# Block means of the values in four column strips, row units finished block by block, and a new order of work, in an attention and feed-forward kernel

## The chip, the cores and the metric

One core of one Trainium2 chip. The metric is the device time of an execution in microseconds; the times shown are of repeated executions, the profile is of one execution.

## What is computed

The reference, cut to what matters:

```python
def _attn_ref(q, k, v):                      # (2, 8, 768, 64) each
    block, window = (32, 16)
    k_sum = k.reshape(B, H, nb, block, D).max(axis=3)
    v_sum = v.reshape(B, H, nb, block, D).mean(axis=3)
    scores_l = scale * np.matmul(q, k.transpose(0, 1, 3, 2))
    mask_l = np.abs(pos[:, None] - pos[None, :]) < window
    scores_s = scale * np.einsum('bhsd,bhnd->bhsn', q, k_sum) + np.log(block)
    scores_all = np.concatenate([np.where(mask_l, scores_l, -1e9), scores_s], axis=-1)
    a = np.exp(scores_all - np.max(scores_all, axis=-1, keepdims=True))
    a = a / (np.sum(a, axis=-1, keepdims=True) + 1e-09)
    return np.matmul(a, np.concatenate([v, v_sum], axis=2))

def reference(...):
    x = attn_out.transpose(0, 2, 1, 3).reshape(1536, 512)
    g = x @ w_gate                                           # 512 x 1536
    x = (g / (1 + np.exp(-g)) * (x @ w_val)) @ w_out         # 1536 x 512
    h = x @ w2_in                                            # 512 x 2048
    h = np.where(h >= 1, h, np.where(h <= -1, 0.0, (h + 1) ** 2 / 4))
    return h @ w2_out                                        # 2048 x 512
```

So each query sees the keys within 16 positions and one summary per block of 32 keys; the summary of the values is their mean. Two feed-forward layers follow. The weights are stored in 64 bits and are decoded on the chip.

## The kernel before

The 1,536 tokens are three chunks of 512. Chunk 0 is the first two thirds of batch 0; chunks 1 and 2 hold the rest of batch 0 and batch 1. Heads go in four pairs (p).

**Attention** runs by pair and segment of 256 queries: windows of 96 keys and 24 block summaries stand beside each other in `kwin`, so one small matmul gives 120 scores. The steps of a segment are a row of jobs (`STAGES`): `sc` scores on TensorE, `mx` maxima on DVE, `ex` exponentials on ACT, `iv` and `no` normalise, `wt` transposes (tile pt), `pt` copies them (pT), and `av` (`values`, tile px) makes the output of a pair for a chunk. Keys are transposed by `kprep` (pk), queries by `queries` (pq). Where a segment is "wide" (the first `T["wide"]` of them), one exponential covers all four windows and the shift and sums lie on DVE or POOL; else there are four exponentials on ACT. **The means of the values** come from `vmean` (L473): for batch 0 TensorE sums eight windows (`wavg`) and two remaining tiles (`tavg`, loaded by `load_vrest`), ten matmuls for each pair, a job `vm` for each; for batch 1 DVE sums each pair (`vsum`, L468, from `load_vb`) and one matmul finishes it. `vmean_out` copies the 24 x 128 result out, and `vmean_put` spreads it to the four windows of a segment, twice a pair; `av` waits for that.

**Feed-forward.** Products are done in three passes of high and low parts (`PASSES`, `mm3`, L942). Chunk 0 runs through both layers while the weights stream in: a pack of gate and val columns (or of two row units of w_out) is loaded (`raw`), decoded on ACT and DVE (L851, L398, L860), written back to DRAM (`kept`) for later and split into high and low parts (`wA`, L398 and L883). Chunks 1 and 2 are then done together: their column products (tiles qg, qv, qi) use seven forms instead of eight (`FORMS`), and their row products add up in four accumulators y0 to y3 (acc_y), one for each block m of 128. Per layer, all row units f of chunk 1 come first, then those of chunk 2 (`row_jobs`, L1301); a unit does its four blocks one after the other, three 512-column matmuls each. When a chunk's last unit ends, the blocks are copied out: in layer 1 as `yf` (ACT), from which DVE and ACT make the operands of layer 2 (`term_jobs`), in layer 2 to `o` and to DRAM (`put`, `store`, L1027).

**What sets the order.** A planner (`Plan.emit`) places all jobs, one after the other, from a table of numbers `T` (ranks and weights), from the durations that each job names, and from rings of buffers. Each engine then runs its list strictly in that order. Where TensorE would sit idle ahead of a job by the plan, up to ten dummy transposes are put in (`bank`, L296; tile names of the next job, with `ident` alone). All DMAs are issued from SP's queue.

```python
job(("vm", *n), {"PE": 2.2}, t + T["vm"], lambda e, tag: vmean(b, p, tag), ...)       # batch 0
job(("vs", *n), {"DVE": 1.95}, t + T["vs"], lambda *_: vsum(b, p), [("vl", *n)], ...) # batch 1
parts = [(m,) for m in range(KK)] if f == LAST[st] else [(0, 1), (2, 3)]              # row_jobs
```

Of the kernel before, what the change touches and what calls it, by code (L numbers as in the profile page):

```python
# [25 lines left out]
 'urge': 0.0031,  # L26
 'weight': (0.111, 25.399, 0.152, 0.551),
# [3 lines left out]
 'd': (-150.471, 8.098),  # L31
 'load': 18.322,
 'high': 36.678,
 'bits': -9.454,
 'keep': -148.441,
 'read': 301.8,
 'hi': 32.014,
 'lo': 24.389,
 'head_rank': (12.184, 257.325, -210.322, -90.628),
 'start': 65.744,  # L40
 'unit': 2.695,
 'e0': 0.54,
 'a1': (48.053, 1.417),
 'a2': (116.684, 4.853),
 'x': (243.217, 367.077),
 'j': (286.932, 586.062),
 'g': (18.981, 22.593),
 'q': (7.889, 10.225),
 'jr': (169.54, 56.215),
 'jw': (46.283, 26.068),  # L50
 'rw': 1.779,
 'js': (52.141, 283.132),
 'gh': (-149.709, 6.427),
 'gl': 43.009,
 't': -14.215,
 'th': 46.02,
 'tl': -107.144,
 'qp': (2.087, 7.089, 2.273, 9.57, 10.813, 5.604, 7.309),
 'qf': 58.875,
 'qj': -17.592,  # L60
 'qa': 36.904,
 'rs': 40.405,
 'rh': -47.821,
 'x2': 1.227,
 'r2': (-57.746, 112.465),
 'first': (7.961, 21.848),
 'st_q': 10.793,
 'st_qt': -84.924,
 'st_kw': 105.468,
 'st_sc': -56.597,  # L70
 'st_mx': -46.073,
 'st_ex': -56.638,
 'st_iv': -145.71,
 'st_no': 96.909,
 'st_wt': 16.772,
 'st_pt': -59.816,
 'st_av': 6.306,
 'st_xh': -15.454,
 'st_xl': -142.311,
 'kl': -35.186,  # L80
 'kp': 2.73,
 'kt': -15.509,
 'km': 49.836,
 'kc': 98.781,
 'vl': 18.792,
 'vm': -50.669,
 'vs': 47.148,
 'vo': -7.827,
 've': 61.456,
 'ql': -1.492,  # L90
 'wl': 12.107,
 'wide': 8,
 'st_sb': 50.586,
 'st_su': 12.78,
 'seg': 41.24,
 'ko': -84.315}
# [135 lines left out]
def tile_block_attention_ffn(  # L232
# [20 lines left out]
    nc = tc.nc  # L253
# [27 lines left out]
    SLOTS = [f"s{i}" for i in range(22)]  # L281
    XS, XF, US = tuple(SLOTS[:8]), tuple(SLOTS[8:16]), tuple(SLOTS[20:22] + SLOTS[8:16])
    JS = tuple(SLOTS + ["kord", "vb"])
    BANKS, ACCS = ("b0", "b1", "b2", "b3"), ("y0", "y1", "y2", "y3")
    plan = Plan({
        **{r: 1 for r in (*BANKS, *ACCS, *SLOTS)}, "kraw": 2, "kord": 1, "vb": 1, "vr": 1,
# [18 lines left out]
    avg = const.tile([P, NB], F32, name="avg")  # L305
# [26 lines left out]
    averages(avg, 4, NB, 0)  # L332


# [6 lines left out]
    averages(tavg[:, NB:NB + P // BLOCK], BLOCK, P // BLOCK, 0)  # L341
# [113 lines left out]
    SUM_ON_PE = (0,)  # L455
    HELD = 2
    NREST = (S - HELD * SEG) // P

    def load_vrest(b):
        t = vraw[b] = sp.tile([P, NREST, H, D], F32, tag="vb", name="vrest", bufs=1)  # L460
        for j in range(NREST):
            src = v[b, 0, HELD * SEG + j * P]
            nc.sync.dma_start(
                out=t[:, j], in_=bass.AP(src.tensor, src.offset, [[D, P], [S * D, H], [1, D]]))

    def vsum(b, p):
        vr = ap_.tile([4 * NB, 2, D], F32, tag="vr", name="vr", bufs=1)
        nc.vector.tensor_reduce(  # L468
            vr, vraw.pop((b, p)).rearrange("p h t d -> p h d t"), axis=AX.X, op=ALU.add
        )  # L470
        pend["vr", b, p] = vr

    def vmean(b, p, tag):  # L473

        pv = bank(tag, "pv")
        if b in SUM_ON_PE:
            parts = []
            for i in range(HELD * WPS):
# [214 lines left out]
    def head_jobs(b, p, t, banks, after):  # L693
# [720 lines left out]
```

## Time and profile before

| what | us |
|---|---|
| median of 3 runs | 623.97 (622.71 to 625.88) |
| the profiled execution's own time | 623.72 |
| its span, first to last instruction | 621.7 |
| busy: TensorE / weight loads / DVE / ACT / POOL | 607.8 / 494.8 / 486.8 / 364.1 / 96.0 |
| chain that ended last: TensorE's share | 86% |

The span is what the profile sees of the execution; the time has some 2 us more around it. A matmul's record lasts longer than its pace (0.39 us against 0.227 for 512 columns), because matmuls are pipelined; pace is read from the distance of starts. An fp32 matmul that isn't a transpose has two records, one of the split parts has one. Line numbers are those of the kernel before; after the change the same statements stand some 4 to 25 lines higher.

### The profile page before, as it was taken

To read this page: it belongs to the slowest core of one execution; us is meant where nothing else is said; L and a number is where in the kernel's file an instruction comes from. 1 tells how busy PE (TensorE), PEld (TensorE's weight loads), DVE (VectorE), ACT (ScalarE), POOL (GpSimd) and SP (SyncE) were. 2 spreads that over 40 slices of the span, in tenths; PEclk is the share of its full clock that TensorE was granted. 3 is DMA by queue.
4 is the path that set the end of the run, shared out by engine and by line. 5 is a ranking of instruction groups with operands and counts; after the bars stand their busy time and mean duration, and the time that the engine had idled before them with its cause. 6 is when DMAs were issued, how large, how long until landed. Compare 5 with 4: busy or idle time off the path is not lost.

```text
span 621.7 us, 9356 instructions
## 1 busy us (share of the span) xinstructions
PE 607.8 (98%) x3473; PEld 494.8 (80%) x3473; DVE 486.8 (78%) x861; ACT 364.1 (59%) x616; POOL 96.0 (15%) x117
## 2 busy tenths in 40 slices
PE   8798999999999999999999999999999999999997
PEld 6676787777878888888888888888877888888886
DVE  5768998798789898997888875777698788765662
ACT  3698879788787895445454442333177756763222
POOL 6453503241311000003220111000001001000000
PEclk9899999999999999999999999999999999999999
DMA  9999999599993963432111101243200031013411
GB/s 218 293 288 305 266 374 343 186 307 307 328 333 114 371 237 118 153 138 66 69 67 69 67 1 68 69 169 103 99 20 20 0 136 34 2 34 123 148 35 67
DMA packets 76749, 95.50 MB, mean 154 GB/s; under 512 B 36256, under 2 KB 58784, under 8 KB 76704
## 3 DMA queue, kind: packets, MB, share of 16 engines
q1 hardware_dynamic: 76704, 94.91, 47.5%
q8 instruction: 27, 0.44, 0.3%
q14 instruction: 18, 0.15, 0.1%
HBM read 73.92 MB, written 20.97 MB: 153 GB/s over the span
## 4 chain that ended last, share of the span: by engine, by line
PE 86%; DMA 7%; DVE 3%; ACT 3%; issue 1%; SPq 1%; ACTq 0%; DVEq 0%
PE acc_y L942 35%; PE qi L942 11%; PE qv L942 9%; PE qg L942 9%; PE pi L942 7%; DMA raw<-in_moe_w_val_dram 5%; PE pg L942 3%; PE pv L942 3%; DMA qraw<-in_q_dram 2%; PE sc L610 2%; PE pv L486 1%; PE pt L666 1%; PE px L560 1%; PE pq L544 1%; ACT dd L851 1%; ACT dd L398 1%
## 5 line engine op out<-in xcount | busy, mean ns | idle before, releaser
L942 PE MATMUL acc_y<-dd,h 128*128 128x512 f32 x384 | 88.0, 389 | 0.0
L942 PEld LDWEIGHTS acc_y<-dd,h 128*128 128x128 f32 x384 | 72.1, 188 | 15.0
L942 PE MATMUL acc_y<-h,dd 128*128 128x512 f32 x288 | 65.6, 389 | 0.0
L942 PEld LDWEIGHTS acc_y<-h,dd 128*128 128x128 f32 x288 | 54.1, 188 | 11.2
L883 POOL TENSOR_TENSOR wjs<-sj,wjs 128x1024 fp32r<-128x1024 f32 x7 | 17.2, 2456 | 286.6 <-ACT wjs L398 240.6
L398 ACT ACTIVATE dd<-wf 128x1024 fp32r<-128x1024 f32 x23 | 24.3, 1059 | 52.8 <-PE acc_y L942 52.7
L942 PE MATMUL acc_y<-wA,h 128*128 128x512 f32 x192 | 46.0, 390 | 0.0
L942 PE MATMUL qi<-xj,wjs 128*128 128x512 f32 x192 | 45.9, 390 | 0.0
L860 DVE SCALAR_TENSOR_TENSOR wb<-dd 128x1024 int32<-128x1024 int32 x34 | 43.4, 1286 | 2.6 <-ACT dd L398 2.1
L942 PE MATMUL pi<-y,wA 128*128 128x512 f32 x128 | 43.5, 396 | 0.0
L942 PEld LDWEIGHTS qi<-xj,wjs 128*128 128x128 f32 x192 | 36.0, 188 | 7.5
L942 PEld LDWEIGHTS acc_y<-wA,h 128*128 128x128 f32 x192 | 35.9, 188 | 7.5 <-issue 0.2
L851 ACT ACTIVATE dd<-raw 128x1024 f32<-128x1024 f32 x34 | 39.1, 1151 | 4.6 <-DMA raw<-in_moe_w_out_dram 2.9
L883 DVE TENSOR_TENSOR h<-r,h 128x512 fp32r<-128x512 f32 x48 | 33.4, 702 | 3.3 <-ACT h L398 1.9
L942 PE MATMUL acc_y<-h,wA 128*128 128x512 f32 x144 | 35.9, 397 | 0.0
L942 PE MATMUL qi<-xj,wjo 128*128 128x512 f32 x144 | 35.6, 391 | 0.0
L942 PE MATMUL qg<-xj,wjs 128*128 128x512 f32 x144 | 35.6, 389 | 0.0
L942 PE MATMUL qv<-xj,wjs 128*128 128x512 f32 x144 | 35.6, 389 | 0.0
L942 PE MATMUL pg<-x,wA 128*128 128x512 f32 x96 | 34.8, 407 | 0.0
L883 DVE TENSOR_TENSOR dd<-wf,dd 128x1024 fp32r<-128x1024 f32 x28 | 34.1, 1222 | 0.5 <-ACT dd L398 0.4
L883 DVE TENSOR_TENSOR wA<-wb,wA 128x1024 fp32r<-128x1024 f32 x28 | 33.9, 1221 | 0.2
L942 PE MATMUL pv<-x,wA 128*128 128x512 f32 x96 | 34.1, 399 | 0.0
(164 smaller groups left out, 1286.6 us busy)
## 6 DMA issues: line engine op xcount, KB each, us to landing
raw<-in_moe_w_out_dram SPq DMA_DIRECT2D x14, 1024.0 KB, 7.7
raw<-in_moe_w_in_dram SPq DMA_DIRECT2D x16, 512.0 KB, 6.1
wf<-kept_z SPq DMA_DIRECT2D x16, 512.0 KB, 3.2
raw<-in_moe_w_gate_dram SPq DMA_DIRECT2D x12, 512.0 KB, 8.1
raw<-in_moe_w_val_dram SPq DMA_DIRECT2D x12, 512.0 KB, 9.0
kept_g<-wb SPq DMA_DIRECT2D x12, 512.0 KB, 7.6
wj<-kept_g SPq DMA_DIRECT2D x12, 512.0 KB, 5.0
wf<-kept_o SPq DMA_DIRECT2D x12, 512.0 KB, 3.3
```

What stands on the lines that cost most here:

```text
L398: nc.scalar.activation(out, in_, AF.Copy, scale=scale)
L486: nc.tensor.matmul(pv[KW:KN, 0:2 * D].rearrange("p (h d) -> p h d", h=2), w, x[:, 2 * p:2 * p + 2], start=i == 0, stop=i == len(parts) - 1,)
L544: nc.tensor.transpose(pq[:, r * P:(r + 1) * P], raw[:, r].rearrange("p h d -> p (h d)"), ident)
L560: nc.tensor.matmul(px[h * D:(h + 1) * D, col:col + QT], vwin[0:KN, w, 2 * p + h], pT[0:KN, 2 * h + w // 2, w % 2 * QT:(w % 2 + 1) * QT], s ...
L610: nc.tensor.matmul(scs[h][j * QT:(j + 1) * QT, w // 2], qT[head, (w + j) * QT:(w + j + 1) * QT], kwin[p][head, w + j], start=True, stop=Tr ...
L666: nc.tensor.transpose(pt[0:KN, w * P:(w + 1) * P], v_["sm"][:, w], ident)
L851: nc.scalar.activation(x[:, 0], raws[k][:, :, :, 1].bitcast(F32), AF.Prelu, scale=2.0 ** -112, alpha=2.0 ** 32)
L860: nc.vector.scalar_tensor_tensor(b, x[:, 0], 3, x[:, 1], op0=ALU.logical_shift_left, op1=ALU.bitwise_or)
L883: e.tensor_tensor(out, a, b, op=ALU.subtract)
L942: nc.tensor.matmul(dst, lhs(a), rhs(b), start=first and i == 0, stop=last and i == 2, **more)
```

## The change

1. The means of a batch are one job `vm`, for all four pairs. Pair p writes to partitions 32p to 32p + 23 of one bank, so its weights (24 columns) go to the p-th strip of 32 columns, and the loop over pairs is the inner one: consecutive matmuls go to different strips. Batch 0 has ten parts as before (40 matmuls), batch 1 eight parts (four windows of one segment and two double tiles of two halves, 32 matmuls) instead of DVE's sums. `load_vb`, `vsum`, `avg` and the tile `vb` go; the remaining tiles come in pieces of four heads into slots of the ring (two for batch 0, four for batch 1).
2. Of chunk 2, the last three row units of each layer are done block by block: block 0 of all three, then block 1, and so on. The very last unit's last block is done in two halves of 256 columns, each copied and stored by itself.
3. The list of durations names 0.92 instead of 1.48 us for `mx`, 1.53 instead of 2.32 for `ex` and other small ones; the number of wide segments is 4 instead of 8; nearly all numbers of `T` are others; two more slots in the ring.

The diff, cut:

```diff
- 'urge': 0.0031,
- 'weight': (0.111, 25.399, 0.152, 0.551),
+ 'urge': 0.00046,
+ 'weight': (0.253, 64.023, 0.063, 0.152),
...
- 'wide': 8,
+ 'wide': 4,
...
-    averages(tavg[:, NB:NB + P // BLOCK], BLOCK, P // BLOCK, 0)
+    averages(tavg[:, NB:NB + 2 * P // BLOCK], BLOCK // 2, 2 * P // BLOCK, 0)
...
+    HELD = (2, 1)
+    HALVES = 2
+    def rests(b):
+        return [(at, x) for at in range(HELD[b] * SEG, S, 2 * P) for x in range(HALVES)]
+    def load_vrest(b, rings):
+        n = H // HALVES
+        for (at, x), ring in zip(rests(b), rings):
+            t = vraw[b, at, x] = slot(ring, "vrest").rearrange("p (h t d) -> p h t d", h=n, d=D)
             nc.sync.dma_start(
+                out=t.rearrange("p h t d -> p h (t d)"),
+                in_=v[b, x * n:(x + 1) * n, at:at + 2 * P].rearrange("h (p t) d -> p h (t d)", t=2),
+            )
+    def vmean(b, tag):
+        pv = pend["pv", b] = bank(tag, "pv")
+        parts = []
+        for i in range(HELD[b] * WPS):
+            at = NB - i * QT // BLOCK
+            vwin = vwins[(b * NSEG + i // WPS) % 2]
+            parts.append((
+                wavg[0:KW, min(i, 1), at:at + NB],
+                lambda p, vwin=vwin, i=i: vwin[0:KW, i % WPS, 2 * p:2 * p + 2]))
+        for at in range(HELD[b] * SEG, S, 2 * P):
+            n = NB - at // BLOCK
+            for t in range(2):
+                parts.append((tavg[:, n:n + NB], lambda p, at=at, t=t: vraw[b, at, 2 * p * HALVES // H][
+                    :, 2 * p % (H // HALVES):2 * p % (H // HALVES) + 2, t]))
+        for i, (w, x) in enumerate(parts):
+            for p in range(NPAIR):
                 nc.tensor.matmul(
-                    pv[KW:KN, 0:2 * D].rearrange("p (h d) -> p h d", h=2), w,
-                    x[:, 2 * p:2 * p + 2], start=i == 0, stop=i == len(parts) - 1,
+                    pv[32 * p:32 * p + NB, 0:2 * D].rearrange("p (h d) -> p h d", h=2), w, x(p),
+                    start=i == 0, stop=i == len(parts) - 1, skip_group_check=True,
                 )
...
-        copy(engine, t[KW:KN], pend["pv", b, p][KW:KN, 0:2 * D])
+        copy(engine, t[KW:KN], pend["pv", b][32 * p:32 * p + NB, 0:2 * D])
...
-        ("mx", {"DVE": 1.48}, T["st_mx"], ("sc",)),
+        ("mx", {"DVE": 0.92}, T["st_mx"], ("sc",)),
...
-        ("ex", {"ACT": 2.32}, T["st_ex"], ("mx",)),
+        ("ex", {"ACT": 1.53}, T["st_ex"], ("mx",)),
...
+        if p == 0:
+            m = len(rests(b))
+            job(("vl", b), {"DMA": (0.45 * m, 0.75 * m, m)}, t + T["vl"],
+                lambda _, *rings: load_vrest(b, rings), (), (XF,) * m, after=after)
+            job(("vm", b), {"PE": (2.85, 2.2)[b]}, t + T["vm"], lambda e, tag: vmean(b, tag),
+                [("vl", b)] + [("wl", b, s) for s in range(HELD[b])], (banks,),
+                [(("vl", b), i) for i in range(m)])
...
-        parts = [(m,) for m in range(KK)] if f == LAST[st] else [(0, 1), (2, 3)]
-        for i, ms in enumerate(parts):
-            name = ("row", c, st, f, i)
+    def row_jobs(c, st, fs, t):
+        todo = [(f, (m,), None) for m in range(KK) for f in fs]
+        if len(fs) == 1 and fs[0] != LAST[st]:
+            todo = [(fs[0], ms, None) for ms in ((0, 1), (2, 3))]
+        if (c, st, fs[-1]) == (C2, 2, LAST[2]):
+            todo[-1:] = [(*todo[-1][:2], half) for half in range(2)]
...
-        for f in range(n):
-            row_jobs(C2, st, f, t0 + UNIT * f)
+        for f in range(n - END):
+            row_jobs(C2, st, [f], t0 + UNIT * f)
+        row_jobs(C2, st, [*range(n - END, n)], t0 + UNIT * (n - END))
```

How the order moves, at three places.

TensorE, around the means of batch 0 (pv with wavg and tavg; ident alone is a dummy; px values, pt transposed weights, pq queries, sc scores, pg the first gate product). Before, from the last pair's means on:

```order
L486 MATMUL pv<-big_135,wavg 24x128 x8
L486 MATMUL pv<-vrest,tavg 24x128 x2
L666 MATMUL pt<-ident,big_134 120x128 x4
L610 MATMUL sc<-big_134,big_135 64x120 x8
L560 MATMUL px<-pT,big_135 64x64 x16
L666 MATMUL pt<-ident,big_134 120x128 x8
L610 MATMUL sc<-big_134,big_135 64x120 x16
L296 MATMUL px<-ident 128x128 x2
L560 MATMUL px<-pT,big_135 64x64 x16
L544 MATMUL pq<-ident,qraw 128x128 x4
L666 MATMUL pt<-ident,big_134 120x128 x4
L942 MATMUL pg<-x_625,wA 128x512
```

After, from the means of all pairs on:

```order
L477 MATMUL pv<-big_131,wavg 24x128 x32
L477 MATMUL pv<-vrest,tavg 24x128 x8
L593 MATMUL sc<-big_130,big_131 64x120 x8
L296 MATMUL px<-ident 128x128 x4
L543 MATMUL px<-pT,big_131 64x64 x16
L649 MATMUL pt<-ident,big_130 120x128 x8
L593 MATMUL sc<-big_130,big_131 64x120 x8
L296 MATMUL px<-ident 128x128 x3
L543 MATMUL px<-pT,big_131 64x64 x16
L593 MATMUL sc<-big_130,big_131 64x120 x8
L649 MATMUL pt<-ident,big_130 120x128 x8
L296 MATMUL px<-ident 128x128 x5
```

Behind these stand one more px, pq, pt, pq and then the first pg. Three values steps come ahead of the first gate product instead of two, and twelve dummies instead of two; the same groups pq, pk, pq, pt, sc stand between the third pair's queries and the means in both, and 11 dummies (5 and 6, with a pt group between) ahead of those queries instead of 10.

ACT, in the same stretch (big<-pv copies of the means, 24x4x128 their broadcasts, mx exponentials, dd a weight's decoding, wA its high part, x the attention output). Before:

```order
L398 ACTIVATE big_135<-pv 24x128
L398 ACTIVATE big_135<-big_135 24x4x128
L635 ACTIVATE big_134<-big_134 128x4x120
L851 ACTIVATE dd<-raw 128x1024
L398 ACTIVATE big_135<-pv 24x128
L398 ACTIVATE dd<-raw 128x1024
L398 ACTIVATE big_135<-pv 24x128
L398 ACTIVATE big_135<-big_135 24x4x128 x2
L851 ACTIVATE dd<-raw 128x1024
L398 ACTIVATE pT<-pt 120x512
L398 ACTIVATE big_135<-pv 24x128
L398 ACTIVATE big_135<-big_135 24x4x128 x2
```

After:

```order
L394 ACTIVATE big_131<-pv 24x128 x4
L394 ACTIVATE big_131<-big_131 24x4x128 x2
L626 ACTIVATE big_130,mx<-big_130,mx 128x120 x4
L394 ACTIVATE x_559<-px 128x512
L394 ACTIVATE pT<-pt 120x512 x2
L826 ACTIVATE dd<-raw 128x1024
L626 ACTIVATE big_130,mx<-big_130,mx 128x120 x4
L394 ACTIVATE x_644<-px 128x512
L394 ACTIVATE pT<-pt 120x512 x2
L394 ACTIVATE wA<-wb 128x1024
L826 ACTIVATE dd<-raw 128x1024
L394 ACTIVATE x_718<-px 128x512
```

The four copies of means stand together, behind the last of the means; single exponentials of the third and fourth pair stand between the copies that the first products need.

TensorE, at the border of the two joint layers (acc_y_4256 and acc_y_4288 are block 2, acc_y_4257 and acc_y_4289 block 3 of chunk 2's rows; qi the first column products of layer 2). Before:

```order
L942 MATMUL acc_y_4241<-h,dd 128x512 x3
L942 MATMUL acc_y_4242<-h,dd 128x512 x3
L942 MATMUL acc_y_4256<-h,dd 128x512 x3
L942 MATMUL acc_y_4257<-h,dd 128x512 x3
L942 MATMUL qi<-xj_4236,wjo 128x512 x3
L942 MATMUL qi<-xj_4266,wjo 128x512 x3
```

After:

```order
L917 MATMUL acc_y_4270<-h,dd 128x512 x9
L917 MATMUL acc_y_4271<-h,dd 128x512 x9
L917 MATMUL acc_y_4288<-h,dd 128x512 x9
L917 MATMUL acc_y_4289<-h,dd 128x512 x9
L917 MATMUL qi<-xj_4278,wjo 128x512 x3
L917 MATMUL qi<-xj_4298,wjo 128x512 x3
```

Each block's nine matmuls of the last three units stand together. Behind the 24 products on wjo, the order before has nine dummies ahead of the products on wjs, the order after has none. The program's end has the same form, with the last nine matmuls as six of 512 and six of 256 columns.

## Rows read from the trace of the kernel before

**Rows 1.** The page: TensorE's busy time, and the DMA engines' share in 40 slices.

```profile
PE 607.8 (98%) x3473; PEld 494.8 (80%) x3473; DVE 486.8 (78%) x861; ACT 364.1 (59%) x616; POOL 96.0 (15%) x117
...
DMA  9999999599993963432111101243200031013411
```

**Rows 2.** Stretches: length, busy PE, PEld, DVE, ACT, POOL, granted clock, DMA share, GB/s.

```profile
16.50:19.77 3.27, 0.03 (x2) 0.04 (x1) 2.42 (x5) 1.32 (x4) 2.51 (x5) 1.00 1.02 199
19.77:24.25 4.48, 4.48 (x42) 3.50 (x43) 2.74 (x4) 3.10 (x7) 2.28 (x3) 0.62 0.92 259
...
40.00:60.00 20.00, 18.37 (x188) 13.75 (x187) 15.06 (x42) 16.78 (x33) 9.49 (x10) 1.00 1.02 309
```

**Rows 3.** Waits of TensorE: total us, times, longest us.

```profile
PE pq L544 <- DMA qraw<-in_q_dram: 4.3, 2, 3.2
...
PE sc L610 <- ACT xf L398: 0.7, 1, 0.7
```

**Rows 4.** The chain that ended last, in order of time: start us, us, what.

```profile
24.09 8.96 PE pv L486 x80
...
33.63 0.57 PE sc L610 x16
34.20 1.08 PE px L560 x32
...
106.69 2.94 PE pv L942 x12
...
137.58 0.87 PE pt L666 x8
...
217.74 2.72 PE pi L942 x12
```

**Rows 5.** Groups of instructions by shape: busy us, mean ns of one, idle before.

```profile
L851 ACT ACTIVATE dd<-raw 128x1024 f32<-128x1024 f32 x34 | 39.1, 1151 | 4.6 <-DMA raw<-in_moe_w_out_dram 2.9 <-DMA raw<-in_moe_w_val_dram 1.6
...
L883 DVE TENSOR_TENSOR wA<-wb,wA 128x1024 fp32r<-128x1024 f32 x28 | 33.9, 1221 | 0.2
...
L398 ACT ACTIVATE wA<-wb 128x1024 fp32r<-128x1024 f32 x22 | 23.2, 1059 | 3.6 <-PE acc_y L942 2.6 <-DVE wb L860 1.0
...
L560 PEld LDWEIGHTS px<-pT,big 120*64 120x64 f32 x384 | 12.2, 138 | 4.0 <-issue 2.7 <-ACT pT L398 0.6 <-ACT dd L398 0.4
...
L398 ACT ACTIVATE x<-px 128x512 fp32r<-128x512 f32 x4 | 2.4, 603 | 0.1
...
L398 ACT ACTIVATE big<-pv 24x128 f32<-24x128 f32 x8 | 2.2, 271 | 3.7 <-PE pv L486 2.7 <-PE pv L493 0.8
```

**Rows 6.** ACT in order of time, a segment's first exponential and what follows them.

```profile
43.80 0.43 ACT L643 ACTIVATE big<-big,mx 128x120 f32<-128x120 f32 x1
...
45.32 0.61 ACT L398 ACTIVATE big<-pq 128x512 f32<-128x512 f32 x1
```

**Rows 7.** TensorE in order of time: start us, us, line, shapes, [idle before <- releaser].

```profile
40.02 0.48 PE L942 MATMUL pg<-x,wA 128*128 128x512 f32 x1
...
48.99 0.38 PE L493 MATMUL pv<-vr,avg 96*24 96x128 f32 x2 [1.49 <-DVE mx L653]
49.30 0.50 PE L942 MATMUL pv<-x,wA 128*128 128x512 f32 x1
...
57.63 0.50 PE L942 MATMUL pg<-x,wA 128*128 128x512 f32 x1
```

**Rows 8.** DVE in order of time: batch 1's sum, a weight's low part, last unit's h.

```profile
46.95 1.89 DVE L468 TENSOR_REDUCE vr<-vb 96x128 f32<-96x1024 f32 x1 [2.98 <-DMA vb<-in_v_dram]
...
53.13 1.21 DVE L883 TENSOR_TENSOR wA<-wb,wA 128x1024 fp32r<-128x1024 f32 x1
...
609.82 0.43 DVE L402 CAST h<-r 128x512 fp32r<-128x512 f32 x1 [0.40 <-PE acc_y L942]
610.28 0.69 DVE L883 TENSOR_TENSOR h<-r,h 128x512 fp32r<-128x512 f32 x1
```

**Rows 9.** All engines in order of time, border of the two joint layers.

```profile
449.65 2.64 ACT L398 ACTIVATE yf<-acc_y 128x512 f32<-128x512 f32 x4 [7.78 <-PE acc_y L942]
...
458.41 1.20 PE L296 MATMUL qi<-ident 128*128 128x128 f32 x9 [1.31 <-DVE qs L1260]
```

More of the change, by code (lines that the diff above doesn't have):

```diff
@@ L30 @@
  'ahead': '',
[L31 to L91, printed above, removed]
- 'wide': 8,
[L93 to L96, printed above, removed]
+ 'd': (513.727, 414.549),
+ 'load': 124.539,
+ 'high': 483.587,
+ 'bits': -209.589,
+ 'keep': 502.954,
+ 'read': 846.482,
+ 'hi': 193.052,
+ 'lo': -262.441,
+ 'head_rank': (358.02, -292.435, 68.215, -43.175),
@@ new lines @@
+ 'start': 54.488,
+ 'unit': 2.713,
+ 'e0': 7.09,
+ 'a1': (51.367, 5.424),
+ 'a2': (84.297, 20.808),
+ 'x': (997.155, 822.108),
+ 'j': (397.141, 1323.573),
+ 'g': (1.056, 60.648),
+ 'q': (1.293, 2.128),
+ 'jr': (63.098, 109.279),
+ 'jw': (346.172, -286.617),
+ 'rw': 824.073,
+ 'js': (-1027.744, 847.579),
+ 'gh': (77.342, -112.509),
+ 'gl': -208.639,
+ 't': 44.334,
+ 'th': 717.665,
+ 'tl': -343.786,
+ 'qp': (-42.293, 5.735, 0.676, 39.985, 34.689, 0.884, -19.193),
+ 'qf': -818.554,
+ 'qj': -683.127,
@@ new lines @@
+ 'qa': -87.222,
+ 'rs': -145.012,
+ 'rh': 205.12,
+ 'x2': -163.338,
+ 'r2': (-111.15, -754.497),
+ 'first': (-127.013, -86.35),
+ 'st_q': 157.871,
+ 'st_qt': -282.792,
+ 'st_kw': 339.155,
+ 'st_sc': -18.389,
+ 'st_mx': -441.157,
+ 'st_ex': -16.002,
+ 'st_iv': -692.985,
+ 'st_no': -30.992,
+ 'st_wt': 11.271,
+ 'st_pt': -166.339,
+ 'st_av': 2.91,
+ 'st_xh': -793.528,
+ 'st_xl': -640.774,
+ 'kl': -516.808,
+ 'kp': -63.466,
+ 'kt': 54.565,
+ 'km': -458.409,
+ 'kc': 91.244,
+ 'vl': -33.859,
+ 'vm': -122.246,
@@ L963, in row_product @@
         else:
-            mm3(acc, lambda a: h[:, a, one], lambda b: w[:, b], f == 0, f == LAST[2])
+            done = f == LAST[2] - (half is None and (c, m) == (C2, KK - 1))
+            mm3(acc, lambda a: h[:, a, one], lambda b: w[:, b], f == 0, done, **free)
     def use(n, ms, rings):
@@ L1019, in y_lo, with out_cols, put, store @@
         )
[L1021 to L1033 removed]
+    def out_cols(half):
+        return slice(0, DM) if half is None else slice(half * DM // 2, (half + 1) * DM // 2)
+    def put(c, m, half, engine, ring):
+        cols = out_cols(half)
+        o = us[c, "out", m, half] = slot(ring, "o")[:, cols]
+        copy(engine, o, accs[c, 2, m][:, cols])
+    def store(c, m, half):
+        r0 = c * CH + m * P
+        nc.sync.dma_start(out=out[r0:r0 + P, out_cols(half)], in_=us[c, "out", m, half])
+    def put_jobs(c, m, t, last, acc, slots, half=None):
+        n = (c, m, half or 0)
+        part = 1 if half is None else 0.6
+        job(("put", *n), {"ACT": 0.61 * part, "DVE": 0.7 * part}, t + 0.65 * m,
+            lambda e, ring: put(c, m, half, e, ring), [last], (slots,), [acc])
+        job(("store", *n), {"DMA": (0.37, 0.75 * part, 1)}, t + 0.65 * m + 0.6,
+            lambda *_: store(c, m, half), [("put", *n)], (), [(("put", *n), 0)])
     where = {u: n for n, u in enumerate(units)}
```

132 lines of the change are left out of this document (42 added, 90 removed).

## The prediction

> **What bounds the kernel now.** I read the page's busy times and slices first: TensorE is busy in 98% of the span, while the DMA engines are at their limit only in the first seven of 40 slices [rows 1]. The table by stretches shows how little TensorE idles even in the busiest time of the others (1.6 of 20 us from 40 on) and what clock it was granted [rows 2]. So time goes where TensorE's own work goes, plus a few gaps; another engine counts only where TensorE then waits. The list of waits names gaps: q transfers 4.3 us in two pieces, ACT before a score 0.7 [rows 3]; two more are shown below. The chain of waits gives the pieces at TensorE's pace: the means of batch 0 stand in it with 8.96 us for 80 records (two for each fp32 matmul), 112 ns each; twelve 512-column products take 2.72 us, 2.94 when a small group stood ahead of them [rows 4].
>
> **The change, part by part.** Durations are those of the profiled run, 623.72 us with a span of 621.70; it lies 0.25 under the median of the runs, 623.97.
>
> *1. Means of batch 0.* The same 40 matmuls now go round four column strips. No row shows four strips with these shapes. Nearest rows: values (px), two column strips over the same rows, 32 records in 1.08 us, 34 ns each; scores, four tiles, 16 records in 0.57 us, 36 ns; above them stands the old 112 ns [rows 4]. In the px group weight loads of 138 ns each pass at that spacing of 34 ns, so loads of one strip do run beside the other [rows 5]. I take 35.6 ns: 80 x 35.6 = 2.85 us, 6.1 us less; the bound above is 8.96. [...]
>
> *2. What the saved 6.1 us become.* Both orders put the same five groups (pq, pk, pq, pt, sc) between the q transfer's landing and the means, so these start at 24.0 again [rows 4] and end at 26.9. Then cover is gone: before, a pair's mean left while the next pair was summed; now none is complete before the last round, and what stood behind must wait for ACT. In its new order ACT does 4 mean copies (4 x 0.27), 2 broadcasts (taken as 512-column copies, 2 x 0.60), four exponentials (43.80 to 45.32: 1.52), an x copy (0.60), two pT copies (1.20), a weight decode (1.15), four exponentials (1.52), an x copy (0.60), two pT copies (1.20): 10.1 us [rows 5, 6]. The third values step then takes TensorE 1.08, and pq, pt, pq 3 x 0.44 (half of the two pt groups' 0.87 [rows 4]): the first gate product starts at 26.9 + 10.1 + 2.4 = 39.4. The other branch (weight copy 1.06, then its remainder on DVE 1.22 [rows 5]) ends at 39.3. That is **0.6 us** earlier than 40.02 [rows 7], not 6.1. The rest isn't all lost: one values step, two pt and one pq more now stand ahead of the first product, 1.08 + 0.87 + 0.44 = **2.4 us** that TensorE does not do later.
>
> *3. Means of batch 1.* Removed: four single matmuls on TensorE (0.31 us each to what follows, 1.2 [rows 7]) and four reductions on DVE of some 1.9 us [rows 8]. Added: 64 records x 35.6 = 2.28 us on TensorE: **+1.1 us**, all on the path, since TensorE is hardly idle there; upper bound 64 x 112 = 7.2. The DVE time itself shortens nothing, but one reduction held DVE for 2.98 us on its transfer, and the mean matmul behind it kept TensorE for **1.49 us** [rows 7, 8]; that wait goes. On SP the batch's transfers are issued ahead of the third gate/val pack instead of one by one later: 1.05 MB, at 309 GB/s [rows 2] 3.4 us of delay for that pack, which before was split by 54.34 and used at 57.63 [rows 7, 8]; in the new order its use comes 33 products and five small groups after 39.4, at about 51. I cost this at nothing, because the pack was late at DVE, which stood behind the held reduction until 48.8; if that cover is not enough, it is rival 3.
>
> *4. Order of the small groups.* After the first product the old order breaks into the stream of products 41 times, the new one 36 times (counted in the two orders). A break costs 2.94 - 2.72 = 0.22 us: **-1.1 us**. The 0.71 us wait of a score [rows 3] stood in a place that the new order doesn't have: **-0.7**. In return the new lists of ACT and DVE will have waits of their own; ACT gets four more segments with single exponentials (1.52 for 0.60), DVE fewer steps. Between none and the 4.5 us of gaps that the old order has after 40 us (1.49, 0.71 and 2.3 below), I put **+1.2**, near the single waits of these rows. The list's new duration of 1.53 us agrees with the 1.52 above; it changes the order alone.
>
> *5. Rows block by block.* At the border of the two joint layers TensorE has 24 products (5.44 us) that need only the first half's results, then sat 1.31 us idle and ran nine dummy transposes, 9 x 0.11 [rows 4, 9]: **2.3 us**. It waited for a DVE chain that begins with the four yf copies from 449.65 on, 0.66 us apart, because the four blocks end 0.68 apart [rows 9]. With the last three units done block after block, three blocks end 6.1, 4.1 and 2.0 us ahead of the last, so most of the chain lies beside products, and the new order has no dummies there. I take all 2.3 off; bounds 1.1 and 2.3. A price: the third unit's h is due 6 products (1.36 us) after the block begins, not 24. Its slot comes free as the block begins; cast and remainder run from 609.82 to 610.97 [rows 8], so 0.1 us is missing with the handoff, in two places, inside the +1.2.
>
> *6. End.* The last copy is 256 columns, not 512. A copy of 128 columns takes 0.27 and of 512 0.60 [rows 5], so 256 take about 0.38: **-0.2 us**; the last transfer is half as long, worth between nothing and 0.2; I take **-0.1**.
>
> Sum: -0.6 - 2.4 + 1.1 - 1.5 - 1.1 - 0.7 + 1.2 - 2.3 - 0.3 = -6.6 us; 623.7 - 6.6 = **617.1 us**.
>
> **Own bounds.** [...] Above: the first product at 41 (a POOL or DVE step late), half of the border kept, 2.5 us of waits: 621.5.
>
> **Rivals.**
>
> *R1, the strips queue.* If a strip's weight load can't pass the matmuls of another strip over the same rows, the pace stays at 112 ns. Then the first block ends at 33.0 and the ACT list follows it unshortened (+6.1), and batch 1 costs 7.2 for 2.3 (+4.9): 628 us, slower. It decides from 6.9 us over the forecast on, that is from 35.6 + 6900/144 = 84 ns a record. The px group speaks against it, though with two strips of 64 columns. [...]
>
> *R2, the front is bound by latency.* The list of step 2 loses another 3 to 4 us, since each values step waits for two segments through DVE, POOL and ACT: first product at 42 to 43, 620.5 us. For it: ACT is busy 16.8 of 20 us between 40 and 60, DVE 15.1 [rows 2].
>
> *R3, the weights come late.* The DMA share is 1.0 in the first 109 us [rows 1, 2]. Counted in products, the third to fifth packs are wanted 5 to 8 us earlier than before; if their transfers aren't, TensorE waits 4 us: 621 us. Against it: the third pack was late at DVE, and from the sixth pack on the new order wants packs 2 to 3 us later than the old one, since more attention stands ahead.
>
> **How the numbers follow.** Forecast 0.68, R1 0.06, R2 0.17, R3 0.09. A measurement can tell some 0.5%, 3.1 us: faster is under 620.9. The forecast lies there, and of R2 and R3 0.14: 0.82; slower is R1, 0.06; the same has 0.12. The range 613.5 to 621.5 holds the forecast with its bounds and most of R2 and R3; R1 and the tails are left out.
>
> **What would show it.** Right: the means in two blocks of about 2.9 and 2.3 us; the first gate product at 38 to 41 us; no dummies and under 0.5 us idle between the joint layers; TensorE's idle time after 40 us near 1 us. Wrong: 80 records still in 9 us (R1); the first product after 42 (R2); TensorE waiting for a weight's remainder between 45 and 95 us (R3); a new wait for the h of a last unit.

## The result and the profile after

The changed kernel takes **616.28 us** (median of 4 runs, 615.53 to 616.86) beside 624.3 for the kernel before in the same set (4 runs, 622.71 to 625.88): ratio **0.987, 95% interval 0.984 to 0.990**. The forecast was 617.1 in 613.5 to 621.5, faster at 0.82. The profiled execution took 616.86 us with a span of 614.8; the one before 623.72 and 621.7. So 6.9 us are to be explained, and the forecast's sum was 6.6. One run further down stands apart: the profiled one of e_vlate was granted a clock of 0.56 in the mean and took 1000.65 us, where its other three took 613.8 to 616.04, and is left out.

The page's busy times of the changed kernel, against [rows 1]: TensorE's share stays at 98%, and its busy time fell by 6.5 us.

```profile
PE 601.3 (98%) x3533; PEld 490.1 (80%) x3533; DVE 486.5 (79%) x857; ACT 368.7 (60%) x645; POOL 101.6 (17%) x110
```

Stretches of the changed kernel, columns as in [rows 2]. The first two and the last are the stretches shown there; the third and fourth lie around the new first gate product.

```profile
16.50:19.77 3.27, 2.58 (x23) 2.17 (x22) 3.20 (x8) 2.48 (x5) 2.56 (x4) 1.00 0.92 232
19.77:24.25 4.48, 4.48 (x128) 3.88 (x128) 4.13 (x16) 3.91 (x14) 1.33 (x2) 1.00 0.93 289
34.24:38.58 4.34, 1.94 (x17) 1.23 (x13) 4.26 (x9) 2.28 (x4) 0.02 (x1) 1.00 0.86 222
38.58:42.40 3.82, 3.82 (x12) 2.64 (x10) 1.84 (x4) 3.30 (x11) 0.40 (x1) 0.55 1.08 357
40.00:60.00 20.00, 20.00 (x168) 15.14 (x167) 13.12 (x43) 16.72 (x45) 8.53 (x11) 0.95 1.01 321
```

TensorE now works 2.58 us in the stretch where it had worked 0.03, and the clock behind it is 1.00 for 0.62. From 40 to 60 it has no gap. But a new gap stands at 34.24: 1.94 us of work in 4.34, and then a clock of 0.55 in the mean over 3.82 us (0.50 in each half microsecond from 39.0 to 42.0). The waits of TensorE, against [rows 3], name the gap in their first line. The second line is new: qu is a sum on DVE that a gate form needs.

```profile
PE pq L527 <- DMA qraw<-in_q_dram: 2.3, 3, 1.5
PE qg L917 <- DVE qu L1246: 2.0, 3, 0.7
```

TensorE in order of time, against [rows 4, 7, 9]: the means of batch 0, the q groups and the first products, the means of batch 1, one of the qu waits, the border of the joint layers.

```profile
21.56 1.95 PE L477 MATMUL pv<-big,wavg 96*24 96x128 f32 x64
23.32 0.62 PE L477 MATMUL pv<-vrest,tavg 128*24 128x128 f32 x16
23.87 0.64 PE L593 MATMUL sc<-big,big 64*64 64x120 f32 x16
...
34.70 0.91 PE L527 MATMUL pq<-ident,qraw 128*128 128x128 f32 x4 [0.39 <-DMA qraw<-in_q_dram]
...
37.50 0.41 PE L527 MATMUL pq<-ident,qraw 128*128 128x128 f32 x2 [1.45 <-DMA qraw<-in_q_dram]
38.38 0.44 PE L527 MATMUL pq<-ident,qraw 128*128 128x128 f32 x2 [0.47 <-DMA qraw<-in_q_dram]
38.58 0.62 PE L917 MATMUL pg<-x,wA 128*128 128x512 f32 x1
...
66.36 1.07 PE L477 MATMUL pv<-big,wavg 96*24 96x128 f32 x32
...
68.23 0.65 PE L649 MATMUL pt<-ident,big 128*120 128x128 f32 x4
...
319.00 1.65 PE L917 MATMUL qg<-xj,wjs 128*128 128x512 f32 x6 [0.67 <-DVE qu L1246]
...
447.61 5.60 PE L917 MATMUL qi<-xj,wjo 128*128 128x512 f32 x24
453.05 8.32 PE L917 MATMUL qi<-xj,wjs 128*128 128x512 f32 x36
```

The 80 records of batch 0 take 23.87 - 21.56 = 2.31 us (28.9 ns each) for 8.96, the 64 of batch 1 1.87 (29.2 ns). The q groups wait 0.39 + 1.45 + 0.47 = 2.31 us. At the border 24 products run straight into the next, without idle time or dummies.

Where the 6.9 us come from: the first product is 1.44 earlier (38.58 for 40.02); from there to the end of the last product it is 572.42 us for 577.92, 5.5 less; the tail behind that is 0.07 longer (3.80 for 3.73). The last products end at 604.69 + 6.31 = 611.00 and, before, at 611.66 + 6.28 = 617.94:

```profile
604.69 6.31 PE L917 MATMUL acc_y<-dd,h 128*128 128x512 f32 x30
```

```profile
611.66 6.28 PE L942 MATMUL acc_y<-dd,h 128*128 128x512 f32 x27
```

SP's queue says why the q groups wait: four vrest transfers of batch 1 hold it for 7.0 us ahead of the k and q transfers of chunk 1. The last q transfer, issued at 35.59, landed at 38.34 by the chain that ended last; SP's list, then that piece:

```profile
21.35 7.03 SPq L455 DMA_DIRECT2D vrest<-in_v_dram  x4
28.48 1.05 SPq L409 DMA_DIRECT2D big<-in_k_dram  x1
29.63 3.88 SPq L421 DMA_DIRECT2D qraw<-in_q_dram  x4
...
34.11 1.95 SPq L421 DMA_DIRECT2D qraw<-in_q_dram  x4
```

```profile
35.59 2.75 DMA qraw<-in_q_dram
```

And ACT's end shows the halves of the last block at work:

```profile
608.97 0.60 ACT L394 ACTIVATE o<-acc_y 128x512 f32<-128x512 f32 x1 [1.44 <-PE acc_y L917]
611.09 0.66 ACT L394 ACTIVATE o<-acc_y 128x256 f32<-128x256 f32 x2 [1.52 <-PE acc_y L917]
```

The first half's copy starts 0.09 us after the *second* half's products end (611.00), and the two copies take 0.66 for one of 0.60.

### The profile page after: what moved, and what is told of

It is laid out like the page before. It is cut to its first block, busy times and chain, and to the rows that moved or that the text cites. A ratio compares the mean times of both kernels' runs of the same rounds, so it can differ in the third digit from the quotient of the medians.

```text
span 614.8 us, 9497 instructions
## 1 busy us (share of the span) xinstructions
PE 601.3 (98%) x3533; PEld 490.1 (80%) x3533; DVE 486.5 (79%) x857; ACT 368.7 (60%) x645; POOL 101.6 (17%) x110
## 4 chain that ended last, share of the span: by engine, by line
PE 93%; DVE 4%; ACT 1%; DMA 1%; issue 1%; SPq 0%; ACTq 0%
PE acc_y L917 37%; PE qi L917 12%; PE qg L917 8%; PE qv L917 8%; PE pi L917 7%; PE pg L917 6%; PE pv L917 6%; DVE sj L1137 2%; PE px L543 2%; PE sc L593 2%; PE pt L649 2%; PE pq L527 1%; PE pk L498 1%; PE pv L477 1%; DVE qu L1246 1%
## 5 line engine op out<-in xcount | busy, mean ns | idle before, releaser
L917 PE MATMUL acc_y<-dd,h 128*128 128x512 f32 (+1 forms) x387 | 87.7, 387 | 0.0
L917 PE MATMUL acc_y<-h,dd 128*128 128x512 f32 x288 | 67.0, 389 | 0.0
L394 ACT ACTIVATE dd<-wf 128x1024 fp32r<-128x1024 f32 x26 | 27.4, 1057 | 59.1 <-PE acc_y L917 59.1
L858 POOL TENSOR_TENSOR wjs<-sj,wjs 128x1024 fp32r<-128x1024 f32 x8 | 21.1, 2632 | 193.6 <-ACT wjs L394 187.0
L835 DVE SCALAR_TENSOR_TENSOR wb<-dd 128x1024 int32<-128x1024 int32 x34 | 41.3, 1220 | 1.1 <-ACT dd L394 0.5
L917 PE MATMUL pi<-y,wA 128*128 128x512 f32 x128 | 42.0, 391 | 0.0
L858 DVE TENSOR_TENSOR wA<-wb,wA 128x1024 fp32r<-128x1024 f32 x31 | 40.7, 1322 | 1.5 <-ACT wA L394 0.7
L917 PE MATMUL acc_y<-h,wA 128*128 128x512 f32 x144 | 37.2, 399 | 0.0
L917 PE MATMUL pg<-x,wA 128*128 128x512 f32 x96 | 35.5, 417 | 0.0
L398 DVE CAST h<-r 128x512 fp32r<-128x512 f32 x38 | 16.2, 426 | 22.5 <-PE acc_y L917 22.0
```

Source lines behind the costliest of these rows:

```text
L394: nc.scalar.activation(out, in_, AF.Copy, scale=scale)
L398: nc.vector.tensor_copy(out, in_)
L835: nc.vector.scalar_tensor_tensor(b, x[:, 0], 3, x[:, 1], op0=ALU.logical_shift_left, op1=ALU.bitwise_or)
L858: e.tensor_tensor(out, a, b, op=ALU.subtract)
L917: nc.tensor.matmul(dst, lhs(a), rhs(b), start=first and i == 0, stop=last and i == 2, **more)
```

## The experiments

Twelve kernels (one of them the changed kernel once more), three sets, each set on one chip with its own runs of the kernel before. These took 623.86, 623.19 and 623.4 us (624.3 above), so medians of different sets compare to about 1 us. Where a number is "in the trace", it is of one profiled execution.

### e_serial0 and e_serial1: the strips one after the other

```
-        for i, (w, x) in enumerate(parts):
-            for p in range(NPAIR):
+        for i, (w, x), p in sorted([(*y, p) for y in enumerate(parts) for p in range(NPAIR)],
+                                   key=lambda y: y[2] if b == 0 else 0):
```

This is e_serial0; e_serial1 has `b == 1`.

> The changed kernel with the means of batch 0 taken pair after pair (each strip's ten matmuls in a row) in place of going round the four strips; batch 1 and every list of the other engines stay. Theory (the pace comes from going round the strips): 80 records at 112 ns again, 8.96 us for 2.31; ACT's list behind them follows unshortened, so the first gate product comes at 36.5 + 6.65 = about 43.2 for 38.58, no q wait is left in front of it and its first products run at full clock: 3.0 to 4.6 us slower than the changed kernel, 619.3 to 620.9. Rival A (cover comes back: pairs 0 to 2 leave while the next is summed, so ACT's four copies of 0.27 are mostly hidden): the first product about 42.2, 618.3 to 619.9. Rival B (the pace of 29 ns does not come from the strips but from the new operands and their order): 80 records still in 2.3 us, 616.3.

> The changed kernel with the means of batch 1 alone taken pair after pair; nothing else moves. Theory (strips, and nothing hides this block, since TensorE hardly idles there): 64 records at 112 ns are 7.2 us for 1.87, all on the path: 5.3 us slower, 621.6. Rival A (TensorE is not the bound around 66 us, later waits absorb it): less than 1.5 us slower, under 617.8. Rival B (the pace is not from the strips): 616.3.

Measured: e_serial0 **618.02** us (617.73 to 618.73), ratio 0.990 (0.989 to 0.992); e_serial1 **618.8** (617.25 to 621.03), ratio 0.992 (0.989 to 0.994). TensorE in e_serial0, in order of time:

```profile
21.70 1.93 PE L477 MATMUL pv<-big,wavg 96*24 96x128 f32 x16
23.46 0.28 PE L477 MATMUL pv<-vrest,tavg 128*24 128x128 f32 x1
23.47 0.29 PE L477 MATMUL pv<-big,wavg 96*24 96x128 f32 x1
...
28.77 0.60 PE L477 MATMUL pv<-vrest,tavg 128*24 128x128 f32 x4
29.30 0.64 PE L593 MATMUL sc<-big,big 64*64 64x120 f32 x16
...
40.94 0.48 PE L917 MATMUL pg<-x,wA 128*128 128x512 f32 x1
```

The block takes 7.60 us (95 ns a record), so going round the strips is what brings the pace. Inside a strip records come 110 ns apart (the first 16 in 1.76 us); at each change of strip the next strip's first four run beside the last four (23.46 to 23.81 at the first change), which is why it isn't 112 throughout.

The time moved far less than the block. The trace explains it: the block is 5.3 us longer, the first product 2.36 later (3.05 of the 5.4 us had been lost to the q waits in the changed kernel anyway, which are gone here), and its products run at full clock (1.00 from 40 to 50), 1.5 us less. The span is 0.9 longer. By the medians it is 1.7, below the expected 3.0 to 4.6. The expectation had the block 6.65 us longer instead of 5.3, and the first product without q waits at 36.5, where the list gives 35.5 (step 2 below). Rival A's cover did not come back: from the end of the block to the last values step it is 9.25 us here (29.30 to 38.55) and 9.27 in the changed kernel (23.87 to 33.14).

In e_serial1 the same edit goes through in full in the profiled runs:

```profile
66.59 1.05 PE L477 MATMUL pv<-big,wavg 96*24 96x128 f32 x8
...
72.45 0.65 PE L649 MATMUL pt<-ident,big 128*120 128x128 f32 x4
```

5.86 us for 1.87, 4.0 more, and the profiled span is 4.2 longer; by the medians 2.5, with runs that spread over 3.8 us, of which the profiled one is the slowest. "On the path" holds in the trace; the expected 5.3 took the old 112 ns for 92.

### e_strip2: two strips at a time

The same edit with `y[2] // 2` as the key.

> The changed kernel with the means of batch 0 going round two strips at a time (pairs 0 and 1, then pairs 2 and 3) in place of four. Theory (records of one strip come 110 ns apart, as e_serial0 shows, and strips run side by side): 55 ns a record, 80 records in 4.2 to 4.4 us. Rival (something else than the strip sets the pace, a load of 103 ns that must follow another): 110 ns a record as one after the other, 7.6 us, or 29 ns, 2.3 us.

One run, 615.68 us, so the time says little; TensorE in order of time:

```profile
22.20 1.93 PE L477 MATMUL pv<-big,wavg 96*24 96x128 f32 x32
...
26.28 0.64 PE L593 MATMUL sc<-big,big 64*64 64x120 f32 x16
```

4.08 us, 51 ns a record: 1.93 to 1.95 us hold 16, 32 and 64 records of `wavg` with one, two and four strips. The strips run side by side.

### e_qfirst, e_vlate, e_vlate2: the vrest transfers of batch 1 further back

```
 class Plan:
+    HOLD, held_back = {("vl", 1): ("ql", 1, 1)}, {}
+    def run(self, name, fn, *a):
+        if name in self.HOLD:
+            self.held_back[self.HOLD[name]] = fn, a
+            return
+        fn(*a)
+        for f, x in [self.held_back.pop(name)] if name in self.held_back else []:
+            f(*x)
...
-            fn(engine, *chosen)
+            self.run(name, fn, engine, *chosen)
```

The plan is made as before, and one job's instructions are issued later; e_vlate holds it until `("load", 3)`, e_vlate2 until `("load", 4)`.

> The changed kernel with one step moved on SP's list alone: the four vrest transfers of batch 1 (needed at 66 us) are issued behind the k and q transfers of chunk 1, pairs 0 and 1, in place of ahead of them; the third gate/val pack stays behind both. Theory (the 2.3 us of waits for q before the first product, and the half clock of the nine products after it, come from vrest standing in front on SP): the second q lands about 3 us earlier (34.4 for 37.5), no wait for q over 0.3 us, first gate product at 36.3 to 36.7, nine products in 2.0 us for 3.65: 2.3 to 3.9 us faster, 612.4 to 614.0. Rival A (latency of ACT's list ends last there: q in time, but the first product still after 38): under 0.7 us faster, 615.6 to 616.3. Rival B (q and k landed late because all transfers share the bandwidth, so moving vrest only makes the third weight pack or vrest late): 616 or more.

Measured: **615.15** us (612.98 to 616.36), ratio 0.984 (0.981 to 0.987): some 1 us below the changed kernel for 2.3 to 3.9 expected, and the two intervals overlap. The last q group ahead of the first product starts at 35.48 without a wait; TensorE in order of time, then ACT, then a stretch with its granted clock (0.67, columns as in [rows 2]):

```profile
35.83 0.48 PE L917 MATMUL pg<-x,wA 128*128 128x512 f32 x1
...
48.26 0.69 PE L543 MATMUL px<-pT,big 120*64 120x64 f32 x16 [1.91 <-ACT pT L394]
```

```profile
41.82 1.14 ACT L826 ACTIVATE dd<-raw 128x1024 f32<-128x1024 f32 x1 [2.49 <-DMA raw<-in_moe_w_val_dram]
...
45.04 1.18 ACT L826 ACTIVATE dd<-raw 128x1024 f32<-128x1024 f32 x1 [1.05 <-DMA raw<-in_moe_w_out_dram]
46.12 0.38 ACT L626 ACTIVATE big<-big,mx 128x120 f32<-128x120 f32 x1
```

```profile
48.26:53.40 5.14, 5.14 (x42) 3.78 (x42) 4.70 (x14) 4.78 (x13) 2.69 (x4) 0.67 1.08 328
```

The theory held for its own place: the first product comes 2.75 us earlier, the nine products take 2.26 us (to the score at 38.09) for 3.82 (38.58 to 42.40), no q wait is over 0.4. Then it was given back: ACT's list has two weight decodes ahead of four exponentials; the decodes waited for the packs, and TensorE for the pT behind the exponentials (47.63), 1.91 us. Behind that wait the lower clock is back: 0.67 in the mean over 5.14 us, which costs some 1.7, by estimate (0.33 x 5.14). So of the 2.75 and 1.56 us gained some 3.6 were lost, and the span is 614.3 for 614.8. That is why the next step went past the packs too.

> As e_qfirst, but batch 1's four vrest transfers are issued behind the third gate/val pack and the first w_out pack as well; no other engine's list changes. What e_qfirst showed: q in time, first product at 35.83, but then ACT stood in its list on the val pack (2.49 us) and on the w_out pack (1.05 us) ahead of four exponentials, and a values step (px) waited 1.9 us for their pT. Theory (what was gained in front was lost to packs that vrest had delayed; vrest itself is wanted only at 66 us): both packs land about 3 us earlier, the exponentials at about 43 for 46.1, no px wait over 0.5 us: 1.5 to 2.3 us faster than e_qfirst's trace, about 612.5 to 613.5. Rival (the DMA engines are full, so the delay only moves on to the next packs or to vrest): TensorE waits for pv, a later weight or a later q instead, 614.5 or more.

> As e_vlate, with vrest of batch 1 one gate/val pack and one q further back on SP's list. Theory (vrest has until 66 us): again no px and no q wait, the next pack a little earlier still; same time as e_vlate within 0.5 us, 612 to 613.5. Rival (vrest lands too late for the means of batch 1): a wait of pv for vrest near 66 us, over 1 us.

e_vlate: 613.8, 614.52 and 616.04 us, ratio 0.987 (0.985 to 0.989): the expected 612.5 to 613.5 were missed, and 614.52 is the rival's bound. This order's waits are read in e_best below. e_vlate2: **615.22** (614.89 to 621.18), ratio 0.989 (0.986 to 0.993), above the expected 612 to 613.5. Its profiled run is the slowest one. Its list of waits shows the rival, though the late transfers are the value windows behind vrest, not vrest itself:

```profile
PE pv L477 <- DMA big<-in_v_dram: 4.3, 3, 2.3
```

None of the three lies clear of the changed kernel's 0.984 to 0.990: that the q waits go is seen in the traces, and what they are worth in the time is shown only together with the qu waits, in e_best.

### e_end1: only the last unit block by block

```
-    prior_row, END = [], 3
+    prior_row, END = [], 1
```

> The changed kernel with only the last unit of each joint layer taken block by block, as before the change (the halves of the last block stay); the planner's lists are the same up to the border of the two joint layers and differ behind it. Theory (the border gained by the blocks ending 2 us apart): ten dummy transposes are back at the border, TensorE idles 1.1 to 1.3 us there: 2.3 us slower, 618.6 (bounds 617.4 and 618.6). Rival (the border was gained by the new order of ACT's and DVE's steps there, not by the blocks): within 0.5 us of 616.3.

Measured: **618.09** us (6 runs, 615.27 to 622.83), ratio 0.991 (0.987 to 0.994), 1.8 us above the changed kernel, though the intervals overlap. TensorE at the border, in order of time:

```profile
451.42 1.25 PE L296 MATMUL qi<-ident 128*128 128x128 f32 x10
452.43 0.94 PE L917 MATMUL qi<-xj,wjs 128*128 128x512 f32 x3
454.30 0.50 PE L917 MATMUL qi<-xj,wjs 128*128 128x512 f32 x1 [0.93 <-ACT xj L394]
455.37 6.88 PE L917 MATMUL qi<-xj,wjs 128*128 128x512 f32 x29 [0.57 <-DVE xj L858]
```

The ten dummies (1.01 us to the next row) and 1.50 us of waits are back: 2.5 us, near the 2.3 forecast from [rows 9]. The rest of the order did not take them away without the blocks. Nor did the blocks without the order: e_oldT below has them, and still idled 0.92 us there and ran seven dummies. Behind the border e_end1 is planned anew, so its time holds more than the blocks.

### e_nohalf: the last block in one piece

```
-        if (c, st, fs[-1]) == (C2, 2, LAST[2]):
-            todo[-1:] = [(*todo[-1][:2], half) for half in range(2)]
...
-            done = f == LAST[2] - (half is None and (c, m) == (C2, KK - 1))
+            done = f == LAST[2]
```

> The changed kernel with the last block in one piece: nine 512-column products, one copy, one transfer; nothing else moves. Prediction's item 6: 0.3 us slower than the changed kernel, in the trace a tail (last product's end to the end of the span) of 4.1 us for 3.80. Theory from the trace of after (the first half's copy starts only when both halves are done, and two copies take 0.66 for one of 0.60): tail 3.7 to 3.9, no difference.

Measured: 614.91 us (613.52 to 618.14), ratio 0.988 (0.985 to 0.992), beside 0.987 and 0.990 for the changed kernel in two sets. In the trace the tail is 3.70 us (609.17 to 612.87) for 3.80. The halves bring nothing.

### e_oldT and e_newT: the table and the code apart

e_oldT is the changed kernel with the old table `T`, e_newT the kernel before with the new one.

> The changed kernel with the old table of numbers for the order (the old ranks, eight first segments with wide exponentials for four): strips, blocks and halves stay, the order is planned anew. In its list the stream of products is broken 44 times for 36, one values step less stands ahead of the first product, and seven dummy transposes stand at the border for none. Theory (the prediction's items on order are right: 2.4 for work moved ahead of the first product, 1.1 for breaks, 0.7 for the score's wait, less 1.2 of new waits, and part of the border): 3.0 to 5 us slower than the changed kernel, 619.3 to 621.3. Rival (the order is worth nothing, the strips and blocks carry the gain): within 1 us of 616.3.

> The kernel before the change with the new table of numbers alone (new ranks, four first segments with wide exponentials for eight); means, rows and end as before the change. The changed kernel with the old table took 623.0, as long as the kernel before. Theory A (the new numbers bring the gain by themselves; the parts add): 623.9 - 6.7 = 617.2. Theory B (the numbers fit one program's list of steps and durations, so neither half works without the other): 622 or more.

Measured: e_oldT **623.0** us (10 runs, 621.3 to 626.16), ratio **1.000** (0.9987 to 1.0016). e_newT **633.33** (632.06 to 634.36), ratio **1.017** (1.014 to 1.020). The code alone brings nothing, the table alone costs 10 us, both together bring 7 to 8, so the two can't be priced apart. Theory B holds, and e_oldT lies above its expectation of 619.3 to 621.3.

In e_oldT the first product comes at 35.62, 3.0 us ahead of the changed kernel's. From there to the end of the last product it is 580.16 us for 572.42. Its list of waits shows some of that (of the first line 1.8 us lie there, the other 0.5 ahead of the first product):

```profile
PE px L543 <- ACT pT L394: 2.3, 2, 1.8
...
PE pg L917 <- DVE wA L858: 1.5, 1, 1.5
...
PE qi L296 <- DVE qs L1246: 0.9, 1, 0.9
```

Of the 7.74 us, 2.4 are the work that stands behind the first product again (px, pt, pq), 2.7 more idle time and 2.25 twenty dummies (ten at 40.9, three at 42.5, seven at the border): 7.35. The rest is 0.4: eight more breaks are paid there, but the changed kernel's 1.6 us of half clock are not (PEclk is 9 in all 40 slices of e_oldT's page). e_newT's means of batch 0 take 8.86 us, as before. Its trace is 8.7 us longer than that of the kernel before: the first product comes 1.3 later, TensorE idles 8.1 us behind it for 3.66, and 32 dummies take 4.5 us there for nine in 1.0; the remaining work takes 0.6 less.

### after_again and e_best

after_again is the changed kernel once more. e_best adds to e_vlate's step three more in the same dictionary, `("qp", 1, i, 0, 3): ("row", 1, 1, i - 1, 2, 0)` for i = 2, 3, 4: half a row unit goes ahead of the gate form that waited for qu.

> The changed kernel, unchanged, once more on the chip of the three others of this set. The q transfers before the first product have landed between 33.9 and 37.5 us in the runs so far, so its first product may come anywhere from 36 to 39: 614.5 to 617, three waits of 0.67 us for the sum of a gate group (qu) between 319 and 365 us.

> The changed kernel with two edits of order: batch 1's vrest transfers behind the third gate/val pack and the first w_out pack on SP (as e_vlate), and at three places of the first joint layer the second half of a row product (acc_y, 6 matmuls, its operands 6 us old) ahead of the gate form that waited 0.67 us for a sum on DVE. Theory (each wait ends because TensorE has ready work in hand): qu waits 0 for 2.0 us, no q wait, 2 to 4 us faster than the changed kernel on this chip, 611.5 to 613.5. Rival (the sums come later and the rows' work is only moved: the next form that needs qu waits instead): waits of the same 2 us elsewhere between 319 and 370 us, 613.5 to 615.

Measured on one chip: after_again **615.96** us (6 runs, 614.06 to 619.77), ratio 0.990 (0.987 to 0.993); e_best **611.26** (5 runs, 611.12 to 614.84), ratio **0.983** (0.980 to 0.985). The intervals don't touch: e_best beats both kernels. In after_again's trace the q waits are 1.0 us, the qu waits 2.0; the last q came later than the expectation's 37.5 in two traces, at 38.34 in the changed kernel's and with a wait that ended at 38.66 in e_serial1's. e_best's whole list of waits over 0.25 us behind 30 us is one line (and a px wait of 0.4); the place of the qu wait now reads as the second fence, in order of time (its first row is the end of six products, cut by the window):

```profile
PE pv L477 <- DMA big<-in_v_dram: 1.0, 1, 1.0
```

```profile
315.72 0.61 PE L917 MATMUL acc_y<-h,dd 128*128 128x512 f32 x2
316.18 1.52 PE L917 MATMUL qg<-xj,wjs 128*128 128x512 f32 x6
317.54 2.88 PE L917 MATMUL qv<-xj,wjs 128*128 128x512 f32 x12
```

All 2.0 us of qu waits are gone and none took their place. The first product comes at 35.06 for 37.06 in after_again. What is new is 1.0 us for batch 1's windows. In the two traces the span is 609.07 for 612.01: 2.0 from the front, 2.0 from qu, less the 1.0.

## Why the prediction was right, point by point

The forecast was 0.8 us off and within its range, but several terms were mis-sized and one was missing; they cancelled. The direction and the main terms were right; that the miss is as small as 0.8 is luck.

- **Step 1, means of batch 0.** "I take 35.6 ns": measured 28.9, so 2.31 us for 2.85. The px row that I took has two strips and streams 64 columns, the means have four and stream 128; two strips with 128 take 51 ns (e_strip2), so the two differences offset each other in part, and the row came near.
- **R1** is out: 28.9 ns, far from the 84 from which it decides. In the trace, over the same rows, loads of 103 ns each pass at a spacing of 28.9 ns, and four strips run four abreast.
- **Step 2, the first product.** Forecast 39.4, measured 38.58. The sentence "these start at 24.0 again" failed: they started at 21.56, since the q group ahead began 1.0 us earlier (18.73 for 19.77), and TensorE, at work for 2.58 of the 3.27 us ahead of 19.77 where it had been for 0.03, was granted 1.00 from there to 24.25 for 0.62. The list behind them took 11.65 us for 12.5 forecast (from 23.87; the last values step began at 33.14, and 2.39 behind that the first product stands in e_serial0, where no q is late). So it would have come at 35.5; e_best, without q waits, has 11.67 us there. The missing term is the q wait: 3.05 us later than that, and 1.6 more at half clock (0.55 in the mean over 3.82 us). It differs between executions: in after_again the product is 2.0 us late, at 37.06, and the clock full (1.00 from 37.06 to 39.28).
- **Step 3.** The failed sentence is "3.4 us of delay for that pack ... I cost this at nothing". The vrest transfers were costed against the third pack alone, and that pack was indeed no problem (R3 is out: TensorE is busy without a gap from 40 to 100). But the k and q transfers of chunk 1 stand between the two in the queue, are wanted first, and went uncounted. The means themselves took 1.87 us for 2.28, and the 1.49 wait is gone.
- **Step 4.** Breaks 42 to 36, score wait gone; new waits +1.2 forecast, 2.0 measured (the three qu waits, away from the front). The price of a break was too low. Counted by the distance of starts behind the first product, idle time fell from 3.66 to 2.00 us, dummies from 0.96 to none, the moved groups (px, pt, pq) by 2.5 for the 2.4 forecast, and the means rose from 1.30 to 1.88. What is left, products, key transposes and scores, fell by 1.0 although 1.6 of half clock are in it: 2.6 for the 1.1 forecast. The 48 records of key transposes alone fell from 3.80 to 2.78, as they stand in four groups for seven. That paid for the half clock, by luck. And the split is not a price list: with e_oldT and e_newT the order's share can't be separated from the code's.
- **Step 5** held to a few tenths: 2.3 forecast, 2.5 in the trace of e_end1, 1.8 in its median.
- **Step 6** failed: -0.3 forecast, +0.07 measured. Half a copy is shorter (0.38 us for 0.60), but the first half's copy waits for the block's last product. Whether that is the program's tracking of the accumulator as one tile was not tried.
- **Own bounds.** No run shows a term for the lower end of the range, 613.5. What the traces show in its place: the clock of 0.62 over 4.48 us behind 19.77 cost the kernel before some 1.7 us, by estimate (0.38 x 4.48), and is 1.00 there after the change, but 1.6 us of the same kind appeared at 38.58. With these 1.7 and the 1.2 of new waits off, the forecast gives 614.2; the terms above it give 621.2, not 621.5. The measured time lies inside both. And the DMA share of [rows 1] is 9 in slices 9 to 12 and 14 too, not in the first seven only; the sum does not rest on that.
- **R2** is out by its number (first product after 42), but as soon as q is in time e_qfirst shows its ACT list next in line, held there by late packs, which is R3's cause.

## What to carry to other kernels

Matmuls with narrow weights (24 columns here) should be issued round the column strips, not strip by strip: with one, two and four strips 1.93 to 1.95 us held 16, 32 and 64 records. When a transfer moves up in a queue, those behind it come later (with the four vrest transfers ahead, 7.03 us of SP's queue, the last q of the front landed at 38.34 us in the changed kernel's trace, after 2.3 us of q waits; with them behind, q waits are 0.4 us or less in e_qfirst, e_vlate2 and e_best), and the one to check is the one that is wanted first, not the one that stands next in the argument. And an order tuned for one program was worth nothing, or less, with the other: code and order are to be judged together, and then waits of the new order with other work ready beside them are cheap to remove by hand (here 4.7 us between the medians).

## What was not expected of the hardware

- Records of the means in one column strip keep 110 ns apart with one, two and four strips at work (16 of a strip in 1.76 us in e_serial0, e_strip2 and the changed kernel), and at a change of strip four records of the next run beside the last four of the old one (23.46 and 23.47 in e_serial0).
- With the same queue order TensorE waited for the q of the front for 1.0 us in after_again, 2.3 in the changed kernel's first trace and 2.4 in e_serial1, and the clock behind these waits differed too. Both together fit the 1.0 to 7.6 us between runs of one kernel, though that they are their cause is not shown: in after_again TensorE worked 1.87 of the 3.36 us ahead of the first product and the clock behind it was 1.00; in the changed kernel's first trace 1.94 of 4.34, and it was 0.55. The runs' mean clocks point the same way: e_nohalf took 613.52 to 614.91 us in its three runs at 1.000, and 617.81 and 618.14 in the two at 0.997.
